# A paired load of the first two weight tiles, and merged stores of the state rows' last output tiles

## The chip, the core and the metric

The kernel runs on one core of one Trainium2 chip. The core has five engines that work side by side: PE (TensorE, matmuls; its weight loads are listed apart as PEld), DVE (VectorE), ACT (ScalarE), POOL (GpSimd) and SP (SyncE). Transfers between the chip's memory (DRAM) and the on-chip memory (SBUF, 128 partitions) are issued by SP or by ACT, each on a queue of its own, and are carried out by 16 DMA engines that both queues share. The metric is the device time of one execution in microseconds. The kernel before takes 871.06 us, the median of three runs (870.91 to 871.29).

## The reference

Three layers follow one another. The inputs are x (batch 8, heads 8, 512 tokens, width 64) and a state (8, 8, 32, 64).

```python
# attention both ways between x and the state
a  = softmax(x @ state.T / 8);   xread = a @ state      # 512 rows per batch and head
a2 = softmax(state @ x.T / 8);   sread = a2 @ x         # 32 rows per batch and head
x = concat([xread, sread], axis=2)                      # -> (8, 576, 512) after the heads are joined
# layer 1: normalise, two matmuls with a relu between, residual
x = x + relu(((x - mean) / std * g_ln) @ w_ch1) @ w_ch2 # w_ch1 512 x 2048, w_ch2 2048 x 512
# layer 2: a gate from a causal 5-tap convolution along the rows, times a projection
out = (sigmoid(conv5(x)) * (x @ w_val)) @ w_out
```

The output has 576 rows per batch: 512 token rows and, behind them, 32 state rows. All arithmetic is float32; the two weight matrices of layer 1 reach the kernel as 64-bit numbers and are turned into float32 on the chip.

## The kernel before

**Start.** `load_tile` loads one weight tile (128 partitions, 512 numbers of 8 bytes, 4 KB per partition, 512 KB in all) by `load_raw` (line 561). Lines 965 to 972 issue, on SP, the first-layer tiles 0, 1 and 2, then x of batch 0 (1 MB, 8 KB per partition, line 109), then tile 3; ACT's queue carries the state of batch 0 (lines 102 and 104), g_ln (line 970) and the identity matrix (line 971). Each tile is decoded in two halves: `decode_a` (two ACT instructions, lines 573 and 575) and `decode_b` (three DVE instructions, lines 581, 583 and 585).

**Order of the first work.** From line 1087 on, the order of PE, ACT and DVE is written out by hand. PE first runs `WARM` = 30 matmuls on zeros (`fill`, line 1095), which only keep it busy. ACT decodes tiles 0, 1, 2. DVE finishes tiles 0 and 1, computes the state's coefficients (lines 125 and 128), finishes tile 2, and only then turns the scores of batch 0 (lines 221 and 225, which need x) and takes their softmax (lines 233 to 235). After that it finishes tile 3. PE runs 14 more fill matmuls behind the scores and then the column sums over tiles 0 to 3 (`colsum`, line 207). The sums are copied by ACT (line 211) and lead into the first hidden layer (lines 169, 170, 729).

**Steady part.** The batches then go through layer 1 in turn (`segment`), with PE as the engine that has nearly no idle time. Behind the eight batches comes one more segment (index B) that holds the state rows of all batches, 256 rows in two tiles of 128. Layer 2 goes over the same nine segments.

**End.** `out_steps(B)` writes the state rows. Row tile 0 holds batches 0 to 3, row tile 1 batches 4 to 7; in each, 32 partitions belong to one batch. The rows of one batch lie together in DRAM, those of the next batch 576 rows further on. So tile 0 is stored by four transfers of 32 partitions (line 923, alternately on SP and ACT). Tile 1 is computed in two column halves of 256, each evicted by ACT (line 935) and stored by four transfers of 32 partitions (line 938): all on SP for the first half, alternately SP and ACT for the last. The token rows are stored by line 925 in transfers of 512 KB.

Buffers: tiles 0 to 3 go to the four `raw` buffers; the `ahl` buffers (two) are first used by the softmax of batch 0.

Of the kernel before, what the change touches and what calls it, by code (L numbers as in the profile page):

```python
# [11 lines left out]
U32 = mybir.dt.uint32  # L12
# [8 lines left out]
P = 128  # L21
B, H, S, NS, D = 8, 8, 512, 32, 64
DM = H * D
DFF = 4 * DM
KT = DM // P
# [2 lines left out]
BASE = 20000  # L28
HLEAD = 4000
LATE = 500  # L30
WARM = 30
DLEAD = 3000
NQ = 4
QF = NF // NQ
# [10 lines left out]
def tile_kernel(ctx: ExitStack, tc: tile.TileContext, xT, xk, stT, sn, w1, w2, wval, wout, convw, gln, ident, stack, out):  # L45
    nc = tc.nc
# [8 lines left out]
    def sb(shape, dt, tag, bufs=1):  # L55
        cnt[0] += 1
        return main.tile(shape, dt, tag=tag, bufs=BUFS.get(tag, bufs), name=f"{tag}_{cnt[0]}")

    def ps(pool, tag, shape):
        cnt[0] += 1  # L60
        return pool.tile(shape, F32, tag=tag, name=f"{tag}_{cnt[0]}")

    def at_ps(shape):
        return ps(ps_at, "at", shape)
# [12 lines left out]
    def mm3(acc, wh, wl, xh, xl, first, last):  # L77
        nc.tensor.matmul(acc, lhsT=wh, rhs=xl, start=first, stop=False)  # L78
        nc.tensor.matmul(acc, lhsT=wl, rhs=xh, start=False, stop=False)  # L79
        nc.tensor.matmul(acc, lhsT=wh, rhs=xh, start=False, stop=last)  # L80
# [19 lines left out]
    def load_state(b, eng=nc.sync):  # L100
        st_raw = small([P, KT, NS], F32, "st_raw")
        eng.dma_start(out=st_raw, in_=stT[b])
        sn_raw = small([P, 2, D], F32, "sn_raw")
        eng.dma_start(out=sn_raw, in_=sn[b])
        loads[b] = [st_raw, sn_raw]
# [453 lines left out]
    def load_raw(tag, src):  # L559
        r = sb([P, DM, 2], U32, tag)  # L560
        nc.sync.dma_start(out=r, in_=src.bitcast(U32).rearrange("p (n two) -> p n two", two=2))
        return r
# [35 lines left out]
    raws, plain_w2 = {}, {}  # L598

    def load_w1(q):  # L600
        for k in range(KT):
            raws["1", 4 * q + k] = load_raw("raw", w1[q, k])

    def load_w2(f):
        raws["2", f] = load_raw(f"w2_{f}", w2[f * P:(f + 1) * P, :])
# [223 lines left out]
    def ntok(i):  # L829
        return S if i < B else NTS  # L830
# [76 lines left out]
    def out_steps(i):  # L907
        n = ntok(i)
        hls = gvs.pop(i)
        for t in range(n // P):  # L910
            if i == B and t == 1:
                break
            o = ps(ps_mm, "mm", [P, DM]) if t % 2 else at_ps([P, DM])
            ts = slice(t * P, (t + 1) * P)
            for e in range(KT):
                mm3(o, hls[e][:, 0, ts], hls[e][:, 1, ts], wo[e][:, 0], wo[e][:, 1], e == 0, e == KT - 1)
            if t % 2 == 0:
                ob = sb([P, 2, DM], F32, "hid", 2)
            nc.scalar.copy(ob[:, t % 2], o)
            if i == B:  # L920
                for j in range(4):
                    eng = nc.scalar if j % 2 else nc.sync
                    eng.dma_start(out=out[4 * t + j, S:, :], in_=ob[32 * j:32 * j + 32, t % 2])
            elif t % 2:
                nc.sync.dma_start(
                    out=out[i, (t - 1) * P:(t + 1) * P, :].rearrange("(u p) d -> p u d", p=P), in_=ob
                )
            yield
        if i == B:
            for half in range(2):  # L930
                cols, ts = slice(half * 2 * P, half * 2 * P + 2 * P), slice(P, 2 * P)
                o = at_ps([P, 2 * P]) if half else ps(ps_mm, "mm", [P, 2 * P])
                for e in range(KT):
                    mm3(o, hls[e][:, 0, ts], hls[e][:, 1, ts], wo[e][:, 0, cols], wo[e][:, 1, cols], e == 0, e == KT - 1)
                nc.scalar.copy(ob[:, 1, cols], o)
                for j in range(4):
                    eng = nc.scalar if half and j % 2 else nc.sync
                    eng.dma_start(out=out[4 + j, S:, cols], in_=ob[32 * j:32 * j + 32, 1, cols])

    def chain(*gens):  # L940
        for g in gens:
# [16 lines left out]
    def load_tile(kind, j):  # L958
        if kind == "1":
            tag = f"w2_{j + 6}" if j // 4 == 1 else "raw"  # L960
            raws["1", j] = load_raw(tag, w1[j // 4, j % 4])
        else:
            raws["2", j] = load_raw(f"w2_{j}", w2[j * P:(j + 1) * P, :])

    load_tile("1", 0)
    load_state(0, nc.scalar)
    load_tile("1", 1)
    load_tile("1", 2)
    load_x(0)
    nc.scalar.dma_start(out=g_sb.rearrange("p k o -> p (k o)"), in_=gln)  # L970
# [116 lines left out]
    with tc.manual_schedule(engines={mybir.EngineType.PE}):  # L1087
# [5 lines left out]
        def fill(n):  # L1093
            for _ in range(n):
                nc.tensor.matmul(warm_ps, lhsT=warm[:, :P], rhs=warm, start=True, stop=True)

        fill(WARM)
        sc0 = [ps(ps_acc, f"acc{2 + u}", [P, S]) for u in range(2)]
# [40 lines left out]
    with tc.manual_schedule(engines={mybir.EngineType.PE}):  # L1139
        segment(1, 8, NF, S, (2, 0), chain(quiet(2), attention_steps(2)))  # L1140
        for b in range(2, B):
            segment(b, 0, NF, S, (b + 1, 0) if b + 1 < B else None, background(b))
        segment(B, 0, NF, NTS, None, before_phase_b())
        at_prio(clock[0] + 16000)
        run_pending()
        bg = x2_steps(1)
        for _ in val_steps(0):
            next(bg, None)
            next(bg, None)
        for i in range(B + 1):  # L1150
            if i + 2 < B:
                load_x2(i + 2)
            bg = x2_steps(i + 2)
            for _ in chain(val_steps(i + 1) if i < B else (), out_steps(i)):
                next(bg, None)
            for _ in bg:
                pass
# [46 lines left out]
```

## Time and profile before

| | |
|---|---|
| median of three runs | 871.06 us |
| the profiled execution's own time | 870.83 us |
| its span, first to last instruction | 868.9 us |
| PE busy | 862.1 us, 99% of the span |
| DVE, ACT, POOL busy | 587.7, 369.7, 199.4 us |
| DMA: moved, mean rate | 72.80 MB, 84 GB/s |

The page of the profile gives busy times and the chain of work that ended last. For this change two short stretches matter: the first 22 us, read from the timeline, the waits and a table of windows, and the last 7 us, read from the timeline, the DMA view and a table of windows. A timeline line gives the start, the length, the engine (SPq and ACTq are the instruction streams that issue transfers), the line of the program, the operation, the tile written and read, the shape and the count; where an engine stood idle, the idle time and what ended it stand in brackets.

### The profile page before, as it was taken

The numbers are of one execution on the slowest core, as the hardware profiler recorded it, in microseconds if no ns is written. First come the engines' busy times: TensorE is split into PE (matmuls) and PEld (weight loads), VectorE is DVE, ScalarE is ACT, GpSimd is POOL, SyncE is SP. The second block draws the span as 40 slices with busy tenths as digits, with TensorE's granted clock in tenths as the row PEclk, the third lists the DMA queues.
The fourth block names the chain that finished last, engine by engine and source line by source line (L and its number), as shares of the span: only waits on it lengthen the run. The fifth ranks groups of instructions, "written<-read, shape, count | busy, mean of one in ns | idle before, by whom it ended". The sixth has DMA issues, their size and how long they took to land.

```text
span 868.9 us, 12589 instructions
## 1 busy us (share of the span) xinstructions
PE 862.1 (99%) x4941; PEld 661.2 (76%) x4942; DVE 587.7 (68%) x995; ACT 369.7 (43%) x696; POOL 199.4 (23%) x162
## 2 busy tenths in 40 slices
PE   9999999999999999999999999999999999999998
PEld 3367767677777777778777777777899888888886
DVE  6999983874746754563674566353389799988870
ACT  5965942233333332432332343132256465455432
POOL 0020200013135133312513422252201223322100
PEclk9999999999999999999999999999999999999999
DMA  9925200321312221230231103010140212223212
GB/s 360 406 85 154 95 29 0 123 79 51 100 53 77 81 72 42 69 99 19 76 98 52 49 11 67 1 49 1 51 144 2 98 73 97 73 98 97 91 55 73
DMA packets 35643, 72.80 MB, mean 84 GB/s; under 512 B 11904, under 2 KB 20608, under 8 KB 31488
## 3 DMA queue, kind: packets, MB, share of 16 engines
q1 hardware_dynamic: 34816, 71.60, 23.9%
q8 instruction: 39, 0.64, 0.3%
q10 hardware_dynamic: 768, 0.40, 0.2%
q14 instruction: 20, 0.16, 0.1%
HBM read 51.01 MB, written 20.97 MB: 83 GB/s over the span
## 4 chain that ended last, share of the span: by engine, by line
PE 86%; DVE 3%; ACT 1%; DMA 0%; issue 0%; DVEq 0%; ACTq 0%
PE mm L734 18%; PE acc L78 16%; PE acc L79 16%; PE acc L80 16%; PE mm L80 2%; PE mm L78 2%; PE mm L79 2%; PE at L80 2%; PE at L78 2%; PE at L79 2%; PE at L147 2%; PE mm L147 1%; PE at L337 1%; PE acc L397 1%; DVE mb L158 1%; PE at L221 1%
## 5 line engine op out<-in xcount | busy, mean ns | idle before, releaser
L78 PE MATMUL acc<-hid,w 128*128 128x512 f32 (+1 forms) x560 | 212.6, 380 | 0.4 <-DVE x L402 0.2
L79 PE MATMUL acc<-hid,w 128*128 128x512 f32 (+1 forms) x560 | 211.4, 378 | 0.0
L80 PE MATMUL acc<-hid,w 128*128 128x512 f32 (+1 forms) x560 | 211.4, 378 | 0.0
L770 DVE SCALAR_TENSOR_TENSOR hid<-mm,hid 128x512 fp32r<-128x512 f32 (+1 forms) x140 | 91.6, 654 | 156.5 <-ACT hid L763 156.3
L734 PE MATMUL mm<-ahl,m 128*128 128x512 f32 x744 | 194.2, 396 | 0.5
L763 ACT ACTIVATE hid<-mm 128x512 fp32r<-128x512 f32 (+2 forms) x144 | 82.3, 571 | 215.5 <-PE mm L734 196.4
L734 PEld LDWEIGHTS mm<-ahl,m 128*128 128x128 f32 x744 | 137.0, 188 | 47.6 <-DVE mb L158 9.3
L78 PEld LDWEIGHTS acc<-hid,w 128*128 128x128 f32 x560 | 105.3, 188 | 24.7 <-issue 1.7
L80 PEld LDWEIGHTS acc<-hid,w 128*128 128x128 f32 x560 | 105.4, 188 | 20.0
L79 PEld LDWEIGHTS acc<-hid,w 128*128 128x128 f32 x560 | 105.4, 188 | 19.1
L861 DVE SCALAR_TENSOR_TENSOR ahl<-big,cw,ahl 128x511 f32<-128x511 f32 (+3 forms) x128 | 102.1, 843 | 0.3
L74 POOL TENSOR_TENSOR m<-mb,m 128x512 fp32r<-128x512 f32 x50 | 65.0, 1320 | 111.1 <-ACT m L73 111.0
L73 ACT ACTIVATE m<-mb 128x512 fp32r<-128x512 f32 x62 | 39.0, 632 | 80.8 <-DVE mb L158 80.5
L847 POOL TENSOR_TENSOR w<-big,w 128x512 fp32r<-128x512 f32 x24 | 37.9, 1611 | 93.0 <-ACT w L845 93.0
L79 PE MATMUL acc<-w,raw 128*128 128x512 f32 (+1 forms) x144 | 54.3, 377 | 0.0
L80 PE MATMUL acc<-w,raw 128*128 128x512 f32 (+1 forms) x144 | 54.3, 377 | 0.0
L78 PE MATMUL acc<-w,raw 128*128 128x512 f32 (+1 forms) x144 | 54.3, 377 | 0.0
L387 POOL TENSOR_TENSOR rstd<-rstd,nhalf 128x16 f32<-128x16 f32 (+1 forms) x9 | 25.7, 2854 | 114.3 <-DVE rstd L385 114.2
L799 DVE TENSOR_TENSOR t<-acc,t 128x512 f32<-128x512 f32 (+1 forms) x44 | 27.8, 660 | 24.3 <-PE acc L80 24.3
L802 POOL TENSOR_TENSOR x<-t,x 128x512 f32<-128x512 f32 x20 | 25.1, 1287 | 78.7 <-DVE t L799 78.7
L873 ACT ACTIVATE ahl<-ahl 128x512 f32<-128x512 f32 (+1 forms) x36 | 21.6, 608 | 45.6 <-DVE ahl L861 45.3
L902 DVE TENSOR_TENSOR w<-ahl,w 128x512 fp32r<-128x512 f32 (+1 forms) x36 | 30.7, 859 | 13.0 <-ACT w L901 12.8
(202 smaller groups left out, 1258.8 us busy)
## 6 DMA issues: line engine op xcount, KB each, us to landing
w<-in_w SPq DMA_DIRECT2D x20, 512.0 KB, 8.0
big<-in_xT SPq DMA_DIRECT2D x8, 1024.0 KB, 4.9
big<-in_xk SPq DMA_DIRECT2D x8, 1024.0 KB, 5.2
x2d<-x SPq DMA_DIRECT2D x8, 1024.0 KB, 4.2
big<-x2d SPq DMA_DIRECT2D x8, 1024.0 KB, 4.8
out<-hid SPq DMA_DIRECT2D x16, 512.0 KB, 2.8
raw<-in_w SPq DMA_DIRECT2D x12, 512.0 KB, 5.6
a2d<-t SPq DMA_DIRECT2D x48, 64.0 KB, 1.7
```

Of the source, the lines that this page charges most:

```text
L73: a = nc.scalar.activation(hi, src, AF.Copy)
L74: eng.tensor_tensor(lo, src, hi.bitcast(F32), op=ALU.subtract)
L78: nc.tensor.matmul(acc, lhsT=wh, rhs=xl, start=first, stop=False)
L79: nc.tensor.matmul(acc, lhsT=wl, rhs=xh, start=False, stop=False)
L80: nc.tensor.matmul(acc, lhsT=wh, rhs=xh, start=False, stop=last)
L734: nc.tensor.matmul(h, lhsT=m[:, u, w, cols], rhs=ahls[b][:, u, x], start=(i, u) == (0, 0), stop=(i, u) == (2, 1),)
L763: a = nc.scalar.activation(hid[:, 0], h, AF.Relu)
L770: marks["dve"] = nc.vector.scalar_tensor_tensor(hid[:, 1], h, 0.0, hid[:, 0].bitcast(F32), op0=ALU.max, op1=ALU.subtract)
L799: marks["dve"] = nc.vector.tensor_tensor(t, accs[d], rrow, op=ALU.mult)
L847: nc.gpsimd.tensor_tensor(lo, src, hi.bitcast(F32), op=ALU.subtract)
L861: t = nc.vector.scalar_tensor_tensor(g[:, j:], x[:, :n - j], cw_sb[:, k, PAD - j:TAPS - j], g[:, j:], op0=ALU.mult, op1=ALU.add)
L902: a = nc.vector.tensor_tensor(hl[:, 1], gt[:, e], hl[:, 0].bitcast(F32), op=ALU.subtract)
```

## The change

The first two weight tiles come in one transfer: the weights are laid out in DRAM so that one partition's parts of tiles 0 and 1 lie side by side, 8 KB together, and the pair goes to an `ahl` buffer in place of two `raw` ones. The other tiles of this matrix are read from the new layout, still 4 KB per partition. The fill matmuls ahead of the first scores go from 30 to 26. At the end, row tile 0 of the state is stored by one transfer of 128 partitions on SP; of row tile 1, the first half by one transfer of 128 partitions on SP and the last half by two of 64 partitions, one on SP and one on ACT.

```diff
-WARM = 30
+WARM = 26
@@ out_steps
             if i == B:
-                for j in range(4):
-                    eng = nc.scalar if j % 2 else nc.sync
-                    eng.dma_start(out=out[4 * t + j, S:, :], in_=ob[32 * j:32 * j + 32, t % 2])
+                nc.sync.dma_start(out=out[4 * t:4 * t + 4, S:, :], in_=ob[:, t % 2])
...
                 nc.scalar.copy(ob[:, 1, cols], o)
-                for j in range(4):
-                    eng = nc.scalar if half and j % 2 else nc.sync
-                    eng.dma_start(out=out[4 + j, S:, cols], in_=ob[32 * j:32 * j + 32, 1, cols])
+                rows = 2 if half else 4
+                for j in range(0, 4, rows):
+                    eng = nc.scalar if j else nc.sync
+                    eng.dma_start(out=out[4 + j:4 + j + rows, S:, cols], in_=ob[32 * j:32 * (j + rows), 1, cols])
@@ load_tile
-            raws["1", j] = load_raw(tag, w1[j // 4, j % 4])
+            raws["1", j] = load_raw(tag, w1[j // 4, j % 4 // 2, :, j % 2])
...
-    load_tile("1", 0)
+    pair = sb([P, 2, DM, 2], U32, "ahl")
+    nc.sync.dma_start(out=pair.rearrange("p j n two -> p (j n two)"), in_=w1[0, 0].rearrange("p j n -> p (j n)").bitcast(U32))
+    for j in range(2):
+        raws["1", j] = pair[:, j]
     load_state(0, nc.scalar)
-    load_tile("1", 1)
     load_tile("1", 2)
@@ kernel
-        "w1": bits(w1.reshape(KT, P, NQ, S).transpose(2, 0, 1, 3)),
+        "w1": bits(w1.reshape(2, 2, P, NQ, S).transpose(3, 0, 2, 1, 4)),
```

## Rows read from the trace of the kernel before

**Rows 1.** The page: busy share, and shares of the chain that ended last.
```profile
PE 862.1 (99%) x4941; PEld 661.2 (76%) x4942; DVE 587.7 (68%) x995; ACT 369.7 (43%) x696; POOL 199.4 (23%) x162
...
PE 86%; DVE 3%; ACT 1%; DMA 0%; issue 0%; DVEq 0%; ACTq 0%
```

**Rows 2.** Timeline, 0 to 12 us: loads issued, fills, decodes of tiles 0 to 2, scores.
```profile
0.74 1.35 SPq L561 DMA_DIRECT2D raw<-in_w  x3
...
1.28 8.59 PE L1095 MATMUL mm<-m 128*128 128x512 bf16 x30 [1.28 <-DVE m L1090]
...
4.87 0.66 ACT L573 ACTIVATE w<-raw 128x512 f32<-128x512 f32 x1 [1.42 <-DMA raw<-in_w]
4.87 0.34 ACTq L971 DMA_DIRECT2D ident<-in_ident  x1
...
5.09 4.27 PEld L1095 LDWEIGHTS <-m 128*128 128x128 bf16 x20 [0.28 <-issue]
...
5.56 0.43 DVE L581 TENSOR_SCALAR w<-w 128x512 f32<-128x512 f32 x1 [4.34 <-ACT w L573]
...
6.34 0.67 ACT L573 ACTIVATE w<-raw 128x512 f32<-128x512 f32 x1 [0.23 <-DMA raw<-in_w]
...
10.21 0.69 DVE L585 CUSTOM_DVE_ANT_0 w<-raw,w 128x1024 uint16<-128x1024 uint16 x1
...
10.47 1.09 PE L221 MATMUL acc<-big,st_raw 64*32 64x512 f32 x16 [0.61 <-DMA big<-in_xT]
...
11.64 1.31 DVE L225 STREAM_TRANSPOSE t<-acc 128x512 f32<-128x512 f32 x2 [0.73 <-PE acc L221]
```

**Rows 3.** Windows of 1 us: busy per engine, then PEclk, DMA share, GB/s last.
```profile
4.00:5.00 1.00, 1.00 (x4) 0.29 (x2) 0.00 (x0) 0.13 (x1) 0.00 (x0) 1.00 1.08 423
5.00:6.00 1.00, 1.00 (x5) 0.44 (x4) 0.43 (x1) 1.00 (x2) 0.00 (x0) 1.00 1.02 389
...
7.00:8.00 1.00, 1.00 (x7) 0.42 (x5) 0.97 (x3) 0.84 (x3) 0.00 (x0) 1.00 1.01 418
```

**Rows 4.** Timeline, 16 to 19 us: tile 3 on DVE, and what PE and ACT do next.
```profile
16.49 0.69 DVE L585 CUSTOM_DVE_ANT_0 w<-raw,w 128x1024 uint16<-128x1024 uint16 x1
...
17.24 0.30 PEld L207 LDWEIGHTS at<-w,g 128*128 128x128 f32 x2 [0.80 <-DVE w L585]
...
18.38 0.68 ACT L1120 ACTIVATE t<-ident,sbn 128x128 f32<-128x128 f32 x2
...
18.97 0.56 ACT L211 COPY cs<-at 128x512 f32<-128x512 f32 x1
```

**Rows 5.** Windows of 5 us behind it (PE, PEld, DVE, ACT, POOL busy).
```profile
20.00:25.00 5.00, 5.00 (x18) 1.63 (x17) 4.81 (x10) 3.77 (x10) 0.00 (x0) 1.00 1.02 417
25.00:30.00 5.00, 5.00 (x14) 1.82 (x14) 4.33 (x14) 5.00 (x11) 0.00 (x0) 1.00 1.03 409
```

**Rows 6.** Timeline of the end: evictions and stores of the state rows.
```profile
862.84 0.93 SPq L923 DMA_DIRECT2D out<-hid  x2
862.84 0.93 ACTq L923 DMA_DIRECT2D out<-hid  x2
...
864.21 2.72 SPq L938 DMA_DIRECT2D out<-hid  x6
...
865.05 0.37 ACT L935 COPY hid<-at 128x256 f32<-128x256 f32 x1 [0.87 <-PE at L80]
865.46 0.80 ACTq L938 DMA_DIRECT2D out<-hid  x2
```

**Rows 7.** DMA view, 862.8 to 869 us: packets, then issues by size and landing.
```profile
DMA packets 582, 0.54 MB, mean 86 GB/s; under 512 B 193, under 2 KB 449, under 8 KB 582
...
out<-hid SPq DMA_DIRECT2D x6, 32.0 KB, 1.6
```

**Rows 8.** The page, DMA issues: the stores of token rows (line 925).
```profile
out<-hid SPq DMA_DIRECT2D x16, 512.0 KB, 2.8
```

**Rows 9.** Windows of the end; columns as in rows 3.
```profile
861.40:861.90 0.50, 0.50 (x4) 0.42 (x3) 0.00 (x0) 0.00 (x0) 0.00 (x0) 1.00 1.00 373
...
864.00:864.50 0.50, 0.50 (x7) 0.50 (x5) 0.00 (x0) 0.19 (x1) 0.00 (x0) 1.00 1.04 250
...
866.50:867.00 0.50, 0.00 (x0) 0.00 (x0) 0.00 (x0) 0.00 (x0) 0.00 (x0) 1.00 0.58 148
...
868.00:868.90 0.90, 0.00 (x0) 0.00 (x0) 0.00 (x0) 0.00 (x0) 0.00 (x0) 0.95 0.00 0
```

More of the change, by code (lines that the diff above doesn't have):

```diff
@@ L601, in load_w1 @@
         for k in range(KT):
-            raws["1", 4 * q + k] = load_raw("raw", w1[q, k])
+            raws["1", 4 * q + k] = load_raw("raw", w1[q, k // 2, :, k % 2])
     def load_w2(f):
```

## The prediction, made before the result was known

> **What bounds the kernel now.** I read the page first. PE is busy 99% of the span and carries 86% of the chain that ended last; DMA has 0% of it [rows 1]. So the middle of the run is PE's, and the change does not touch it: what comes after the first layer-1 work only moves with its start. Two places are left where this change can make time: the stretch before PE is steadily fed, and the stretch after PE's last matmul. I read them in that order, each from the timeline, and then priced the transfers from the windows and the DMA view.
>
> At the start the reader should see a relay. Tile 0 lands and ACT begins to decode at 4.87; DVE begins at 5.56, and its last instruction of the decode of tile 2 starts at 10.21 and ends at 10.90. It has no gap between. x releases the scores at 10.47 (PE stood idle 0.61), and DVE takes the scores at 11.64 after 0.73 us of idling [rows 2]. So here x is last, and DVE's decode has 0.73 us to spare. From 11.64 DVE runs without a gap until it has finished tile 3, at 16.49 + 0.69 = 17.18, and PE's fourth column sum waits for just that and starts at 17.24 [rows 4]. DVE therefore sets the start of everything behind it.
>
> At the end, PE is done at 865.0, ACT has evicted the last half at 865.42, and ACT issues at 865.46, but SP issues six transfers one after the other from 864.21 for 2.72 us, so its last one starts near 866.5 [rows 6]; it lands 1.6 us later, near 868.1 [rows 7]. The span ends at 868.9. Here SP's issuing is the bound.
>
> **The front: the pair.** Before, ACT and DVE work on tile 0 while tile 1 is in flight. Tile 1 is released at 6.34 [rows 2], and both tiles in one transfer cannot be released before about then. Larger packets help little: x, with 8 KB per partition, moves at 418 GB/s at a DMA share of 1.01, the 4 KB tiles at 389 to 423 at 1.02 to 1.08 [rows 3], which is 414 against some 385 at a full share; that is 0.17 us for 1 MB. I take the release at 6.2. ACT's first decode, and with it DVE's, slips by 6.2 - 4.87 = 1.33 us. DVE's block of 10.90 - 5.56 = 5.34 us then ends at 5.56 + 1.33 + 5.34 = 12.23, past the 11.64 at which the scores are there now (11.5 if x gains its 0.1). DVE loses 0.55 us, its spare time is gone, and what is late is DVE instead of x. ACT is not late: its six decode instructions at 0.67 us [rows 2] end by 10.3, and it then waits for DVE anyway. The ends for this term are -0.1 (only x's gain counts) and +1.33 (nothing is spare); I take +0.55, because the spare time is a row.
>
> Behind it nothing gives the 0.55 us back: tile 3 passes from DVE to PE, then ACT copies the sums at 18.97, with two other instructions just before [rows 4], and in the next windows DVE has 4.81 and ACT 5.00 of 5 us busy [rows 5]. So PE's steady part starts 0.55 us later, and the end with it.
>
> **The front: smaller edits.** One issue less on SP is some 0.45 us (three take 1.35 [rows 2]), but the DMA share is at 1.0 [rows 3], so an earlier issue waits in the queue: nothing. The identity matrix's issue on ACT stands beside the first decode, at 4.87 [rows 2], and may slip with it by 1.33 us; it is read at 18.38 [rows 4], so that is covered. The last twenty fills take 4.27 us, so four fewer are 4 x 0.21 = 0.85 us of PE work [rows 2]; they end at 9.0 in place of 9.87, ahead of a wait for x until 10.4: nothing, and the idle time grows from 0.6 to 1.4 us. The pair's buffer is free again at 10, long before the second use of `ahl`, and tiles loaded later into `raw` find their buffers no later than before: nothing.
>
> **The end: fewer issues.** SP has one issue for the last half in place of two behind four others; it and ACT's start at 865.46. If the merged transfers still run on all 16 engines, each queue brings 4 packets per engine, 8 in all in place of 2. A 1 KB packet takes 1024 B / (148 / 0.58 / 16 GB/s) = 64 ns [rows 9], so six more are 0.4 us, and the last lands at 865.46 + 1.6 + 0.4 = 867.4: 0.7 us sooner than 868.1.
>
> **The end: how many engines.** This is the term that decides, and no row shows it. What the rows show is how the old transfers were dealt out. In the last 6 us there are twelve of 32 partitions, and the packets under 512 B are 193: 16 closings for each of the twelve and one over. The 1 KB packets are 449 - 193 = 256, that is 8 x 32 [rows 7]. So every transfer was closed on 16 engines, with two whole rows on each: whole, equal shares of the outermost count, 32. The merged store has an outermost count in DRAM of 4 batches, and of 2 in the last half. Whole shares of that go to 4 engines and to 2 engines. I take whole shares, since nothing in the trace was dealt any other way; the other end is 16 engines, above.
>
> The price: in full flow an engine moves 373 / 16 = 23.3 GB/s [rows 9], 88 ns for 2 KB; I take 46 ns for 1 KB, a little over half. Row tile 0 is then 32 packets of 2 KB on each of four engines, 2.8 us; the first half 32 packets of 1 KB, 1.5 us. The last half puts 32 packets from SP and 32 from ACT on two engines: 2.9 us if both queues get the same two, and I take it that they do, as the dearer of the two cases that leave a share whole. All of it adds up on those engines, since SP's packets stand in line: 7.2 us. The fixed part of a landing is 2.8 - 16 x 0.088 = 1.4 us, from the 512 KB stores [rows 8]. From the first issue at 862.84 [rows 6] the last landing is at 862.84 + 1.4 + 7.2 = 871.45, against 868.1: +3.35 us. Bounds inside this case: 128 KB per engine if the two last halves lie on different engines, 862.84 + 1.4 + 5.8 = 870.0, so +1.9; and 160 KB at the slow rate of the 32-partition stores, 250 / 1.04 / 16 = 15 GB/s or 68 ns per KB [rows 9], 10.9 us, so +7.0.
>
> The Trainium skill, "DMA: Bandwidth & Descriptors", section "Why a DMA increments its semaphore by 16 and not by 1", says of transfers issued from SP and ACT that the number of engines is the largest one up to 16 that divides the slowest counts of both patterns, and that these are the lowest-numbered engines. The closings of [rows 7] agree for a count of 32; for 4 and 2 no run here shows it. By that rule the sum is the one with 4 and 2 engines, by the same page's rule on small transfers it is the one with 16 (below).
>
> **The sum.** The profiled execution took 870.83 us, 1.93 around a span of 868.9. With +0.55 and +3.35 the span is 872.8 and the execution 874.7; the median of the runs is 0.23 above the profiled one, so 874.9.
>
> **The rivals.** (1) The merged stores run on 16 engines. Then the end gains 0.7 and the front loses 0.55: 870.9, no measurable change and not slower. It decides from about eight engines on: 64 KB each are 2.9 us, landing at 862.84 + 1.4 + 2.9 = 867.1, before the last half's issue allows. For it: the SBUF side still has 128 partitions. Against it: no row of a transfer whose shares were cut. The Trainium skill, "DMA: Bandwidth & Descriptors", section "Rules for kernel authors", speaks for it with its advice to merge small transfers, because under 64 KB most of the time is overhead; the 1.6 us for 32 KB beside 2.8 us for 512 KB agree [rows 7, 8].
>
> (2) The front costs nothing, because the pair lands early enough to fit DVE's 0.73 us: 874.3 with the stores on few engines. It needs the pair by 5.6, when one tile took until 4.87 and the DMA share is already 1.0 [rows 2, 3].
>
> (3) PE's clock falls in the longer idle time before the scores, and the next 3 us of fills and the first column sums run at 1.2 in place of 2.4 GHz: scores 1.1 us later, some 1.7 in all, 876.6. Against it: at the end the granted clock is still 1.00 until the last tenth of 868.0 to 868.9 [rows 9], over 3 us after the last matmul, and here the idle time is 1.4 us.
>
> (4) The order of ACT, DVE and SP behind the hand-written part is planned anew from changed due times; nothing in the trace prices it, and I allow 1 us either way.
>
> **How the numbers follow.** Few engines at the end with the front's loss (with or without rivals 2 and 4): 0.74. Sixteen engines: 0.20. A fallen clock on top: 0.04. Something that gains more than the 0.7 us: 0.02. About 0.2%, 1.7 us, is what a measurement of this kernel can tell from no change. Slower by more than that takes 872.8; the first case passes it but for its low corner (870.0 at the stores, no loss in front), the second does not. Slower 0.74, same 0.22, faster 0.04. The likeliest case alone is 872.9 to 878.3 (bounds +1.9 to +7.0, with the front's); to leave out no more than 2 in 10 the range must reach into rival 1, to 870.7.
>
> **What would show it.** The pair: ACT's first decode near 6.2, DVE taking the scores near 12.2 with no idle time before, PE's fourth column sum near 17.8. The stores: closing packets of the four merged transfers, 4 + 4 + 2 + 2 if I am right and 64 if not; in the windows behind 865 a low DMA share with a long tail; the merged store of tile 0 landing 4 us and more after its issue. I am wrong if the last landing comes within 2 us of the last issue, or if DVE still idles before the scores.

## The result and the profile after

The changed kernel takes 876.79 us (median of six executions, 876.62 to 876.85), against 871.08 us for the kernel before beside it: a ratio of 1.0065 (95% interval 1.0052 to 1.0078), 5.7 us slower. The profiled execution took 876.85 us with a span of 874.9 us; before it was 870.83 and 868.9. The 6.0 us by which the spans differ fall into two parts. PE's last matmul starts at 865.52 in place of 864.74, 0.78 us later, and from there to the end of the span it is 9.38 us in place of 4.16, 5.22 us more.

The page of after: the busy times and the chain that ended last, as in [rows 1].

```profile
PE 860.9 (98%) x4937; PEld 660.7 (76%) x4938; DVE 588.2 (67%) x995; ACT 369.5 (42%) x696; POOL 199.9 (23%) x162
...
PE 86%; DVE 2%; ACT 1%; issue 0%; DVEq 0%
```

PE has four fills less and runs the same instructions otherwise; the chain still is PE's and says nothing of a tail of 9 us that lies in transfers. The page alone would not have shown the cause.

The timeline of after at the start (start, length, engine, line, operation, tiles, idle time and what ended it), to be read beside [rows 2] and [rows 4]:

```profile
6.09 0.66 ACT L573 ACTIVATE w<-ahl 128x512 f32<-128x512 f32 x1 [1.90 <-DMA ahl<-in_w]
...
10.29 1.09 PE L221 MATMUL acc<-big,st_raw 64*32 64x512 f32 x16 [1.27 <-DMA big<-in_xT]
...
12.06 1.31 DVE L225 STREAM_TRANSPOSE t<-acc 128x512 f32<-128x512 f32 x2
...
17.65 1.12 PE L207 MATMUL at<-w,g 128*128 128x512 f32 x2 [0.56 <-DVE w L585]
```

The pair lands at 6.09 and ACT's first decode starts 1.22 us later than before. DVE takes the scores at 12.06 with no idle time in front, and PE's fourth column sum starts at 17.65, 0.41 us later than the 17.24 of [rows 4]. PE keeps this distance until about 100 us. There it grows by 0.84 us. Timeline of after, ACT near 78 us and PE near 101 us:

```profile
78.19 1.29 ACT L73 ACTIVATE m<-mb 128x512 fp32r<-128x512 f32 x2 [3.26 <-DVE mb L158]
79.38 0.58 ACT L763 ACTIVATE hid<-mm 128x512 fp32r<-128x512 f32 x1
...
101.40 1.65 PE L734 MATMUL mm<-ahl,m 128*128 128x512 f32 x6 [0.97 <-DVE hid L770]
```

The same of the kernel before:

```profile
76.04 0.60 ACT L763 ACTIVATE hid<-mm 128x512 fp32r<-128x512 f32 x1 [1.53 <-PE mm L734]
...
78.76 1.14 ACT L73 ACTIVATE m<-mb 128x512 fp32r<-128x512 f32 x2
...
100.15 1.66 PE L734 MATMUL mm<-ahl,m 128*128 128x512 f32 x6
```

Before, ACT ran the relu (L763) first and the two copies `m<-mb` behind it, and PE started the L734 matmuls without a wait. Now the copies stand ahead of the relu on ACT and wait 3.26 us for DVE. Some of the loss comes back later: the distance is 1.25 us at 101 us and 0.78 us at the end.

Timeline of after at the end (line 921 is now the store of row tile 0, line 937 the stores of the halves), beside [rows 6]:

```profile
863.63 0.70 SPq L921 DMA_DIRECT2D out<-hid  x1
...
864.80 1.97 SPq L937 DMA_DIRECT2D out<-hid  x2
...
865.52 0.28 PE L80 MATMUL at<-w,w 128*128 128x256 f32 x1
...
865.84 0.37 ACT L933 COPY hid<-at 128x256 f32<-128x256 f32 x1 [1.06 <-PE at L80]
866.24 1.37 ACTq L937 DMA_DIRECT2D out<-hid  x1
```

PE's last matmul in the kernel before:

```profile
864.74 0.28 PE L80 MATMUL at<-w,w 128*128 128x256 f32 x1
```

Windows of after at the end; columns as in [rows 3], so the last three are PEclk, DMA share and GB/s:

```profile
864.50:865.00 0.50, 0.50 (x6) 0.50 (x6) 0.00 (x0) 0.28 (x1) 0.00 (x0) 1.00 0.04 12
865.00:865.50 0.50, 0.50 (x6) 0.50 (x5) 0.00 (x0) 0.00 (x0) 0.00 (x0) 1.00 0.38 37
865.50:866.00 0.50, 0.30 (x3) 0.10 (x1) 0.00 (x0) 0.16 (x1) 0.00 (x0) 1.00 0.29 12
866.00:866.50 0.50, 0.00 (x0) 0.00 (x0) 0.00 (x0) 0.21 (x1) 0.00 (x0) 1.00 0.07 12
866.50:867.00 0.50, 0.00 (x0) 0.00 (x0) 0.00 (x0) 0.00 (x0) 0.00 (x0) 1.00 0.27 61
...
868.00:868.50 0.50, 0.00 (x0) 0.00 (x0) 0.00 (x0) 0.00 (x0) 0.00 (x0) 1.00 0.26 98
...
871.00:872.00 1.00, 0.00 (x0) 0.00 (x0) 0.00 (x0) 0.00 (x0) 0.00 (x0) 0.50 0.14 48
...
873.00:874.00 1.00, 0.00 (x0) 0.00 (x0) 0.00 (x0) 0.00 (x0) 0.00 (x0) 0.50 0.06 19
```

The DMA share is that of 16 engines, so it counts them. 0.26 x 16 is four engines, at 98 GB/s; 0.14 x 16 is two, at 48 GB/s. Before, the rows of the end show shares of 1.04 (from 864.0) and 0.58 (from 866.5) [rows 9]. From 865.5 to 866.5 only 12 GB/s move, at shares of 0.29 and 0.07. A packet is counted whole in the window in which it starts, so the two are read together: about three engines are occupied for a microsecond, and what moves is an eighth of the 98 GB/s that move later.

DMA view of after from 866 us to the end, beside [rows 7]:

```profile
DMA packets 381, 0.49 MB, mean 55 GB/s; under 512 B 12, under 2 KB 268, under 8 KB 381
```

The packets under 512 B are the closings, 12: four for each of the two 128-partition stores and two for each of the two 64-partition stores.

### The profile page after: what moved, and what is told of

It is laid out like the page before. It is cut to its first block, busy times and chain, and to the rows that moved or that the text cites. A ratio compares the mean times of both kernels' runs of the same rounds, so it can differ in the third digit from the quotient of the medians.

```text
span 874.9 us, 12571 instructions
## 1 busy us (share of the span) xinstructions
PE 860.9 (98%) x4937; PEld 660.7 (76%) x4938; DVE 588.2 (67%) x995; ACT 369.5 (42%) x696; POOL 199.9 (23%) x162
## 4 chain that ended last, share of the span: by engine, by line
PE 86%; DVE 2%; ACT 1%; issue 0%; DVEq 0%
PE mm L734 18%; PE acc L78 16%; PE acc L79 16%; PE acc L80 16%; PE mm L80 3%; PE mm L78 3%; PE mm L79 3%; PE at L80 2%; PE at L78 2%; PE at L79 2%; PE at L147 2%; PE mm L147 1%; PE at L337 1%; PE acc L397 1%; DVE mb L158 1%; PE at L221 1%
## 5 line engine op out<-in xcount | busy, mean ns | idle before, releaser
L770 DVE SCALAR_TENSOR_TENSOR hid<-mm,hid 128x512 fp32r<-128x512 f32 (+1 forms) x140 | 91.7, 655 | 156.3 <-ACT hid L763 156.1
L734 PE MATMUL mm<-ahl,m 128*128 128x512 f32 x744 | 194.1, 396 | 1.3 <-DVE hid L770 1.0
L734 PEld LDWEIGHTS mm<-ahl,m 128*128 128x128 f32 x744 | 137.0, 188 | 48.4 <-DVE mb L158 9.3
L763 ACT ACTIVATE hid<-mm 128x512 fp32r<-128x512 f32 (+2 forms) x144 | 82.2, 571 | 213.4 <-PE mm L734 194.1
L74 POOL TENSOR_TENSOR m<-mb,m 128x512 fp32r<-128x512 f32 x50 | 64.9, 1317 | 111.1 <-ACT m L73 111.0
```

The costliest lines, as they stand in the source:

```text
L74: eng.tensor_tensor(lo, src, hi.bitcast(F32), op=ALU.subtract)
L734: nc.tensor.matmul(h, lhsT=m[:, u, w, cols], rhs=ahls[b][:, u, x], start=(i, u) == (0, 0), stop=(i, u) == (2, 1),)
L763: a = nc.scalar.activation(hid[:, 0], h, AF.Relu)
L770: marks["dve"] = nc.vector.scalar_tensor_tensor(hid[:, 1], h, 0.0, hid[:, 0].bitcast(F32), op0=ALU.max, op1=ALU.subtract)
```

## The experiments

Each experiment is timed beside the kernel before on the same chip; a ratio is that of the medians, with its 95% interval. "PE's distance" is how much later PE starts the same matmul than in the profile of before.

### Front alone, stores alone

`e1_front` is the changed kernel with the stores of the kernel before (lines 921 to 923 and 936 to 938 there); `e2_stores` is the kernel before with the changed stores alone:

```diff
-                for j in range(4):
-                    eng = nc.scalar if j % 2 else nc.sync
-                    eng.dma_start(out=out[4 * t + j, S:, :], in_=ob[32 * j:32 * j + 32, t % 2])
+                nc.sync.dma_start(out=out[4 * t:4 * t + 4, S:, :], in_=ob[:, t % 2])
...
-                for j in range(4):
-                    eng = nc.scalar if half and j % 2 else nc.sync
-                    eng.dma_start(out=out[4 + j, S:, cols], in_=ob[32 * j:32 * j + 32, 1, cols])
+                rows = 2 if half else 4
+                for j in range(0, 4, rows):
+                    eng = nc.scalar if j else nc.sync
+                    eng.dma_start(out=out[4 + j:4 + j + rows, S:, cols], in_=ob[32 * j:32 * (j + rows), 1, cols])
```

> The changed front alone (paired load, 26 fills), with the stores of the kernel before. Theory: DVE, late by the pair, costs 0.4 us at PE's fourth column sum (17.65 against 17.24), and the order of ACT that is planned anew near 75 us another 0.4 us, so PE's last matmul ends near 865.8 against 865.0 and the time is 871.9 us (+0.8). Rival: the front costs nothing and the whole loss of 5.7 us is the stores': 871.1 us.

> The merged stores alone, with the front of the kernel before. Theory (few engines): PE's last matmul ends at 865.0 as before, 12 closing packets in place of 192 for the state's stores, and the end is as late behind PE as in the changed kernel, 9.1 us in place of 3.9: 876.0 us (+4.9 to +5.0). Rival (the stores are only hurt together with the later front): less than +4.

Measured: `e1_front` 871.81 us against 871.24 (1.0007, 0.9998 to 1.0016); `e2_stores` 875.91 us against 871.24 (1.0054, 1.0041 to 1.0068). DMA view of `e2_stores`, 863.5 to 875 us:

```profile
DMA packets 396, 0.52 MB, mean 46 GB/s; under 512 B 12, under 2 KB 268, under 8 KB 396
```

With the old front the tail is the same as in after: 12 closings, and from PE's last matmul (864.73) to the end of the span (874.1) 9.37 us. The two parts add up: +0.6 and +4.7 us, 5.2 of the 5.7. So the stores are the change's cost; the front is small, and its interval reaches below 1.

### Same stores, other rows: is it the engines or the merging?

`e10_rows128` is `e2_stores` with another target. It issues the same four transfers of the same bytes from the same tiles, but into 128 or 64 consecutive token rows, so that the outermost count in DRAM is 128 or 64 in place of 4 or 2. It leaves out the state rows of all eight batches, not only of batches 4 to 7 as its expectation says, and writes over token rows of batches 0 and 1.

```diff
-                nc.sync.dma_start(out=out[4 * t:4 * t + 4, S:, :], in_=ob[:, t % 2])
+                nc.sync.dma_start(out=out[0, :P, :], in_=ob[:, t % 2])
...
-                    eng.dma_start(out=out[4 + j:4 + j + rows, S:, cols], in_=ob[32 * j:32 * (j + rows), 1, cols])
+                    eng.dma_start(out=out[1, 32 * j:32 * (j + rows), cols], in_=ob[32 * j:32 * (j + rows), 1, cols])
```

> The kernel before with the changed stores, but the four merged transfers go to 128, 128, 64 and 64 consecutive rows of token rows in place of the state rows (so the state rows of batches 4 to 7 are left out and token rows are written over): as many issues, as many bytes and as large packets as in the changed kernel, and an outermost count of 128 or 64 in DRAM in place of 4 or 2. Theory (the number of engines sets the price): 64 closings in place of 12, the last landing about 2 us behind the last issue, near 867.5, span 868.2 to 868.6, 870.1 to 870.5. Rival (merging by itself is dear, through longer issues or a late start of the flow): a span of 871 us or more, over 873.

Measured: 870.35 us against 871.09 (0.9991, 0.9981 to 1.0001), span 868.6. DMA view of `e10_rows128` from 862.5 us, the packets and the store of tile 0 with its landing time:

```profile
DMA packets 453, 0.55 MB, mean 90 GB/s; under 512 B 65, under 2 KB 321, under 8 KB 452
...
out<-hid SPq DMA_DIRECT2D x1, 256.0 KB, 2.4
```

Timeline of `e10_rows128`, its first and its last issue:

```profile
862.85 0.34 SPq L921 DMA_DIRECT2D out<-hid  x1
...
865.47 0.56 ACTq L937 DMA_DIRECT2D out<-hid  x1
```

Window of `e10_rows128` behind the store of tile 0; columns as in [rows 3]:

```profile
863.50:864.00 0.50, 0.50 (x6) 0.50 (x6) 0.00 (x0) 0.37 (x1) 0.00 (x0) 1.00 0.60 213
```

The closings are 64 (and one of another transfer). Tile 0 moves at 213 GB/s about a microsecond behind its issue and lands after 2.4 us, and the tail from PE's last matmul is 3.85 us in place of 9.37. Merging is therefore not dear by itself: with 16 engines it is no dearer than the twelve small stores. The gain that the prediction's first rival gave it is not told from none: 0.74 us by the medians with an interval that reaches 1.0001, and 0.31 us by the tails (3.85 against 4.16). What is dear is the small outermost count. The edit changes the pattern in DRAM along with the count, from rows of several batches to plain rows; that the number of engines follows from the count in a plain transfer too is shown by `e7_rows` below. The issuing instruction is shorter as well: 0.34 us on SP for tile 0 in place of 0.70, and 0.56 us on ACT for the last half in place of 1.37.

### Each merged store by itself

`e3_tile0` takes the first half of the edit of `e2_stores` alone: tile 0 in one store. `e4_last` merges the stores of the last half alone:

```diff
-                for j in range(4):
-                    eng = nc.scalar if half and j % 2 else nc.sync
-                    eng.dma_start(out=out[4 + j, S:, cols], in_=ob[32 * j:32 * j + 32, 1, cols])
+                rows = 2 if half else 1
+                for j in range(0, 4, rows):
+                    eng = nc.scalar if half and j else nc.sync
+                    eng.dma_start(out=out[4 + j:4 + j + rows, S:, cols], in_=ob[32 * j:32 * (j + rows), 1, cols])
```

> Only the store of row tile 0 merged (one transfer of 128 partitions, outermost count 4); all of tile 1 stored by 32 partitions as before. Theory: 4 closings for it, its packets flow on four engines, full flow starts only some 2.5 us after the issue, and it closes near 868.1 to 868.9; the later stores have their packets on these four engines behind it, so the span is 869.5 to 870. If the late start of the flow came from the next merged transfer issued behind it, its packets flow from 1.0 us after the issue and close near 866.6, and the span is within 0.3 of 868.9. If it ran on 16 engines: 16 closings, span 868.7.

> Only the last half merged (two transfers of 64 partitions, outermost count 2, one on SP, one on ACT); tile 0 and the first half stored by 32 partitions as before. Theory: 2 + 2 closings, both queues on the same two engines, 64 packets of 46 ns on each, 2.9 us; with a flow that starts 2.5 us after the issue at 865.46 the span is 871.8 (+2.9), with one that starts after 1.0 us it is 870.3 (+1.4). If the queues had different pairs of engines, 1.5 us less. On 16 engines: 868.1 (-0.8).

Measured: `e3_tile0` took 873.5 us in a single execution (before 871.24), with 6.65 us from PE's last matmul to the end and a span of 871.7, where 869.5 to 870 was expected: a miss. `e4_last` took 873.11 us against 871.24 (1.0022, 1.0013 to 1.0031), with 6.75 us and a span of 871.7, where 871.8 was expected. The size was as expected, but the way to it was not quite: SP's merged store is the last of five issues that run from 864.74 to 867.32, and the expectation had it at 865.46. Timeline of `e3_tile0` (line 936 is the stores of the halves):

```profile
863.15 0.70 SPq L921 DMA_DIRECT2D out<-hid  x1
...
864.32 5.20 SPq L936 DMA_DIRECT2D out<-hid  x6
```

DMA view of `e3_tile0`, issues with their landing times:

```profile
out<-hid SPq DMA_DIRECT2D x6, 32.0 KB, 4.4
out<-hid ACTq DMA_DIRECT2D x2, 32.0 KB, 4.0
```

The six small stores on SP now take 5.20 us to issue in place of 2.72 [rows 6], and the 32 KB stores, ACT's too, land 4.0 to 4.4 us after their issue (medians) in place of 1.6 [rows 7]. I read this so: each of them has a share on the engines that still work on tile 0, and has not landed before that share is through. That a transfer on four engines holds up the transfers behind it that use all sixteen is what the landings show. The expectation had this, but not that SP's issuing is held up with them: its 2.48 us more are as much as the tail grew (6.65 - 4.16 = 2.49). Why the issuing takes longer, no row shows.

### The rule for the number of engines, away from the end

`e7_rows` cuts three stores of 128 token rows in the middle of layer 2 into pieces of 124 + 4, 62 + 62 + 4 and 31 + 96 + 1 rows: plain transfers, one row per partition, under other work.

```diff
+                cuts = {3: (0, 124, 128), 4: (0, 62, 124, 128), 5: (0, 31, 127, 128)}.get(i)
+                if cuts and t == 3:
...
+                    for lo, hi in zip(cuts, cuts[1:]):
+                        nc.sync.dma_start(out=out[i, t * P + lo:t * P + hi, :], in_=ob[lo:hi, 1])
```

> A probe in the middle of layer 2, where nothing waits for the stores: the last row tile of batches 3, 4 and 5 is stored by plain two-dimensional transfers of 124 + 4, 62 + 62 + 4 and 31 + 96 + 1 rows, everything else as before. Theory (as many engines as divide the outermost count): closings 4 + 4, 2 + 2 + 4 and 1 + 16 + 1, and 84 to 88 ns per packet of 2 KB on each engine. Two readings of the late flow of the merged stores: if it comes from many rows per engine, these flow late as well, some 1 us after the first packets; if it comes from the three-dimensional pattern of the merged stores, they flow at once. The time stays at 871.1 to 871.4.

Measured: 871.79 us in a single execution; the time is not the point. Windows of `e7_rows` behind the 62-row stores, which are issued from 808.92; columns as in [rows 3]:

```profile
810.00:811.00 1.00, 1.00 (x6) 0.84 (x5) 1.00 (x2) 0.00 (x0) 0.00 (x0) 1.00 0.10 23
...
814.00:815.00 1.00, 1.00 (x6) 0.79 (x6) 1.00 (x2) 0.57 (x2) 0.00 (x0) 1.00 0.14 53
```

DMA view of `e7_rows`, 808.5 to 817 us:

```profile
DMA packets 137, 0.28 MB, mean 33 GB/s; under 512 B 8, under 2 KB 8, under 8 KB 136
```

Windows of `e7_rows`: the first of the 124-row store, two in which the 96-row store flows, and one with the 31-row store alone:

```profile
792.00:793.00 1.00, 1.00 (x6) 0.84 (x5) 1.00 (x3) 0.02 (x1) 0.00 (x0) 1.00 0.25 92
...
825.00:826.00 1.00, 1.00 (x6) 0.80 (x6) 1.00 (x4) 0.00 (x0) 0.00 (x0) 1.00 0.90 250
826.00:827.00 1.00, 1.00 (x6) 0.84 (x5) 1.00 (x3) 0.00 (x0) 0.00 (x0) 1.00 0.30 72
...
828.00:829.00 1.00, 1.00 (x6) 0.84 (x5) 1.00 (x3) 0.00 (x0) 0.00 (x0) 1.00 0.06 25
```

Timeline of `e7_rows`, the issues of the 124 + 4 and of the 62 + 62 + 4 rows:

```profile
787.69 0.68 SPq L929 DMA_DIRECT2D out<-hid  x2
...
808.92 1.15 SPq L929 DMA_DIRECT2D out<-hid  x3
```

The shares count two engines (0.14), four (0.25) and one (0.06): the largest divisors of 62, 124 and 31 up to 16. The closings of the 62 + 62 + 4 rows are 2 + 2 + 4 = 8. So a prime or nearly prime number of rows does the same as a few batches, in a plain transfer too. Two engines need some four microseconds here to come from 23 to 53 GB/s, with their share at 0.10 to 0.14 all the while: the slow start is not owed to the pattern of the merged stores. Nor does it go with few engines alone. The 124-row store, whose bytes moved only some 4 us after its issue, behind a load of 1 MB, ran at 92 GB/s on four engines in its first window. The 96-row store, on 16 engines, was slow: 250 GB/s at a share of 0.90 and 72 at 0.30 are 17 and 15 GB/s per engine, against 23.3 in full flow [rows 9]. In `e10_rows128`, also on 16 engines, tile 0 was not slow. What makes the first packets slow I did not find out. The long issues are not owed to few engines alone either: here two take 0.68 us and three take 1.15, below 0.4 us each on average.

### The front taken apart

`e8_fills30` has the pair and the layout with 30 fills, `e9_fills26` is the kernel before with 26 fills and nothing else; `e5_two_loads` has the layout and the `ahl` buffer with 26 fills, but two loads of 4 KB per partition. All three keep the old stores.

```diff
-    nc.sync.dma_start(out=pair.rearrange("p j n two -> p (j n two)"), in_=w1[0, 0].rearrange("p j n -> p (j n)").bitcast(U32))
-    for j in range(2):
-        raws["1", j] = pair[:, j]
+    def load_half(j):
+        nc.sync.dma_start(out=pair[:, j], in_=w1[0, 0, :, j].bitcast(U32).rearrange("p (n two) -> p n two", two=2))
+        raws["1", j] = pair[:, j]
+    load_half(0)
     load_state(0, nc.scalar)
+    load_half(1)
     load_tile("1", 2)
```

The diff is that of `e5_two_loads` against `e1_front`. `e8_fills30` is `e1_front` with `WARM = 30`, and `e9_fills26` is the kernel before with `WARM = 26`.

> The pair in one transfer, but 30 fills as before; stores as before. ACT's order near 75 us is that of the kernel before. Theory: PE's fourth column sum +0.4 (17.65), no second step near 100 us, PE's last matmul +0.4 or less, 871.5 us. Rival (the second step comes from the pair's late start and not from the order): PE's shift still grows by 0.8 near 100 us.

> The kernel before with WARM = 26 in place of 30 and nothing else. Theory (four fills fewer change the order that is planned for ACT behind the hand-written part, two copies of m<-mb are put ahead of the relu near 76 us): PE shows no shift against the kernel before up to 99 us beyond the scatter of x's landing, a step of about 0.8 us near 100 us, and 0.4 to 0.6 us of it at the end: 871.4 to 871.6. Rival (the pair's loads and the weights' new layout move ACT's order, the number of fills has no part in it): no step near 100 us, 871.0.

> The changed front with 26 fills, the new layout and the pair's buffer, but tiles 0 and 1 in two transfers of 4 KB per partition; stores as before. ACT's planned order near 75 us is that of the changed kernel (two evictions of m ahead of a relu of hid). Theory: tile 0 is released near 4.9 again, DVE takes the scores at 11.64 and PE's fourth column sum starts at 17.24 (+0.0), but the order still costs 0.8 us behind 85 us, of which 0.4 come back by 650: PE's last matmul +0.4, 871.5 us. Rival (the order costs nothing, all of the front's loss is the pair's): 871.1.

Measured: `e8_fills30` 871.05 us against 870.96 (1.0001, 0.9992 to 1.0010); `e9_fills26` 871.84 against 871.09 (1.0010, 1.0001 to 1.0019); `e5_two_loads` 871.85 against 870.96 (1.0011, 1.0002 to 1.0020). The first is lower than expected, the other two are higher, by 0.2 to 0.5 us. Timeline of `e8_fills30`, ACT and PE:

```profile
76.25 0.60 ACT L763 ACTIVATE hid<-mm 128x512 fp32r<-128x512 f32 x1 [1.53 <-PE mm L734]
...
78.98 1.15 ACT L73 ACTIVATE m<-mb 128x512 fp32r<-128x512 f32 x2
...
100.36 1.66 PE L734 MATMUL mm<-ahl,m 128*128 128x512 f32 x6
```

The same of `e9_fills26`, with two lines of DVE:

```profile
78.03 1.29 ACT L73 ACTIVATE m<-mb 128x512 fp32r<-128x512 f32 x2 [3.25 <-DVE mb L158]
...
78.70 1.35 DVE L74 TENSOR_TENSOR m<-mb,m 128x512 fp32r<-128x512 f32 x2
...
79.23 0.58 ACT L763 ACTIVATE hid<-mm 128x512 fp32r<-128x512 f32 x1
...
100.47 0.68 DVE L770 SCALAR_TENSOR_TENSOR hid<-mm,hid 128x512 fp32r<-128x512 f32 x1
...
101.21 1.65 PE L734 MATMUL mm<-ahl,m 128*128 128x512 f32 x6 [0.93 <-DVE hid L770]
```

DVE of the kernel before, the same two places:

```profile
80.97 1.28 DVE L74 TENSOR_TENSOR m<-mb,m 128x512 fp32r<-128x512 f32 x2
...
99.41 0.68 DVE L770 SCALAR_TENSOR_TENSOR hid<-mm,hid 128x512 fp32r<-128x512 f32 x1
```

The number of fills alone puts the copies ahead of the relu. With 30 fills and the pair, ACT's order is that of before, and PE's distance is 0.20 us at 17.5 us, 0.21 at 100 and 0.05 at the end. With 26 fills and the old loads it is 0.25 us at 17.5, 1.06 at 101 and 0.98 at the end. The fills are not slower and are not missed by PE; what costs is that an order that is planned for ACT and DVE came out otherwise 70 us later. In the whole trace of `e9_fills26` this is the one place where the order on PE, ACT, DVE or POOL differs from before, but for the fills: ACT's two copies, and DVE's two instructions behind them (L74), stand ahead of a relu and of an L770. DVE carries the loss on. It is busy for 26.60 of the 27 us from 74 to 101 in the kernel before, so it has nothing to make it up from: its instructions are 0.27 us late at 77.3, 0.84 at 83.6 and 1.06 from 89.7 to 100.47, and the L770 there is what PE waits for. The step goes with this order in every kernel: 0.8 us in the four with 26 fills (after, `e1_front`, `e5_two_loads`, `e9_fills26`), at most 0.1 in the other eight, which have 30.

The profiled execution of `e5_two_loads` was one of two in ten that took about 873 us; the other eight took 871.5 to 871.9. Its timeline at the scores:

```profile
10.84 1.76 PE L221 MATMUL acc<-big,st_raw 64*32 64x512 f32 x16 [2.30 <-DMA big<-in_xT]
```

Windows of `e5_two_loads`; columns as in [rows 3]:

```profile
11.00:12.00 1.00, 1.00 (x16) 0.02 (x3) 0.26 (x1) 0.00 (x0) 0.00 (x0) 0.57 1.01 401
12.00:13.00 1.00, 1.00 (x10) 0.20 (x3) 0.37 (x1) 0.90 (x2) 0.00 (x0) 0.50 1.03 410
```

x came 0.55 us later than in after and the fills ended 0.48 us sooner (8.54 against 9.02), so PE idled 2.30 us, and the granted clock fell to 0.5, from 2.4 to 1.2 GHz, from shortly after 11 us until past 14: the scores took 1.76 us in place of 1.09. PE's distance is 1.88 us at the fourth column sum and 1.5 from 21 us to the step at 100. That is the prediction's third rival. In after, the idle time was 1.27 us and the clock stayed.

### A store order that is no slower

`e6_spread` is the kernel before with the first half's four stores alternately on SP and ACT.

```diff
-                    eng = nc.scalar if half and j % 2 else nc.sync
+                    eng = nc.scalar if j % 2 else nc.sync
```

> The kernel before with the first half's four stores of tile 1 alternately on SP and ACT, as the last half's are; every transfer stays at 32 partitions. Theory: 16 closings for each, SP's last issue starts near 865.9 in place of 866.5, and the span is 868.3, the time 870.6 us (-0.5), too little for the interval to show. Rival: ACT's two more issues delay its last eviction (865.05) or its own issues, and the time is 871.1 or more.

Measured: 870.15 us against 870.96 (0.9992, 0.9983 to 1.0000). Timeline of `e6_spread`:

```profile
864.24 1.74 ACTq L938 DMA_DIRECT2D out<-hid  x4
```

Its span from PE's last matmul is 4.08 us against 4.16, so the profile shows hardly any gain at the end; ACT's four issues now end last, at 865.98. PE's last matmul came 0.82 us earlier in this execution, which the edit does not touch: x landed early, and the scores started at 9.93 in place of 10.47, which is 0.54 of it. It is the lowest time measured, but the interval reaches 1, and it can't be told from the kernel before.

## Why the prediction was right, and where it was off

The direction and the mechanism came out as argued: 876.79 us measured, 874.9 predicted. For the profiled execution the prediction made 874.7; it took 876.85, and the 2.15 us between them are 0.23 at the front and 1.87 at the end, but for rounding. Two of its sums are a little off: 12.23 - 11.64 is 0.59 and not 0.55, and 871.06 + 0.55 + 7.0 is 878.6 and not 878.3. Neither changes a reading.

**What bounds the kernel, and the two places.** Right. No other stretch changed, but for the step at 100 us and the part of it that comes back later.

**The pair.** The steps were right: release at 6.09 (6.2 predicted), scores on DVE at 12.06 without idle time (12.2), fourth column sum at 17.65 (17.8). But 0.41 us in one profile is not a price. In the eight profiles with the old loads (before, `e2_stores`, `e3_tile0`, `e4_last`, `e6_spread`, `e7_rows`, `e9_fills26`, `e10_rows128`) the scores start between 9.93 and 11.18, the fourth column sum 6.76 to 6.78 us behind them, and DVE always idles before the scores, 0.43 to 1.58 us: there the landing ahead of the scores sets the start, and it moves from one execution to the next. The profile of before, with 10.47, is the second earliest of the eight; five of them have the column sum at 17.41 to 17.65. With the pair DVE sets the start, and the column sum is at 17.44 (`e8_fills30`), 17.50 (`e1_front`) and 17.65 (after), no later than those five. `e8_fills30` puts the pair at +0.1 us, with an interval of -0.7 to +0.9. The term of 0.55 failed where it took the spare time of one execution, and an early one, for that of all.

**Fills at nothing.** Wrong: +0.75 us by the medians of `e9_fills26` (0.1 to 1.7 by its interval). The named cover, the wait for x, was there (1.27 us idle), but the cost lay where no row of the front could show it, in the order planned for ACT and DVE. The fourth rival had named that and allowed 1 us either way; 0.8 us of it came true. It stood in for the pair's missing 0.45, so the sum for the front (0.55) was nearly right, by 0.57 us in `e1_front`, by luck and not by its reason.

**Fewer issues.** The gain of 0.7 us, which held for 16 engines only, is not shown: `e10_rows128` is 0.74 us below the kernel before by the medians, but the interval of the ratio (0.9981 to 1.0001) allows no gain too, and the two profiles' tails differ by 0.31 us.

**How many engines.** Right, and the term that decided: 4 + 4 + 2 + 2 closings. The rule of the Trainium skill, "DMA: Bandwidth & Descriptors", section "Why a DMA increments its semaphore by 16 and not by 1", agrees with these 12, with the 64 of `e10_rows128` and with 62, 124 and 31 rows. The Trainium skill's section "Rules for kernel authors" of the same page, by which merging small transfers pays, goes against the +4.7 us of `e2_stores` and fits `e10_rows128` at most. That advice speaks of overhead, so the prediction's 16 engines did not follow from it.

**The price of few engines.** The mis-sized term: +5.22 us in place of +3.35. The rates were right: 98 to 104 GB/s on four engines and 48 on two were measured, 93 and 47 taken (23.3 each). Both last halves did go to the same two engines. The first bytes also moved no later than I took it: 6 KB came before 865.0, within 1.4 us of the issue at 863.63. What failed is the step from the fixed part of 1.4 us, read from 512 KB stores on 16 engines, straight to full flow. From 865.0 to 866.5 the windows carry (37 + 12 + 12) x 0.5 = 31 KB, where 93 GB/s are 140 KB; from 866.5 to 868.0 they carry (61 + 61 + 90) x 0.5 = 106 KB. The 143 KB that lack are 1.5 us at 93 GB/s, of the 1.87 us. The rest, 0.35 us, I can't place. The upper bound of +7.0 held it.

**The rivals.** (1) 16 engines: ruled out by the closings, and `e10_rows128`, which has them, shows no loss. (2) A free front: within the scatter for the pair. (3) The clock: not in after, but in `e5_two_loads` after 2.30 us of idling; PE's lasting distance of 1.5 us there, less the 0.37 us by which x came later than in [rows 2], is 1.1 us, against the 1.7 us that I took. What I held against it, that the clock stayed for over 3 us after the last matmul of before, did not rule it out. (4) The new order: as above.

## What to carry to other kernels

Before merging stores, look at the outermost count of the pattern in DRAM: where it is 4 or 2, the transfer runs on four or two of the sixteen engines, and the DMA share in a table of windows (0.26, 0.14) and the number of closing packets say so at once. A kernel's end has nothing to hide such a transfer, and it also holds up the small transfers behind it that have a share on the same engines, and their issuing. And where a planner orders the instructions, compare the order on each engine after any edit, an edit of idle work included: four dummy matmuls less moved two instructions on each of two other engines 70 us later and cost 0.8 us.

## What the runs showed of the hardware that I had not expected

A store's first packets can be slow. In after, the merged stores carried 12 GB/s from 865.5 to 866.5, at a mean share of 0.18, and 98 GB/s from 868.0 on; in `e7_rows` two engines came from 23 to 53 GB/s in some four microseconds, and 16 engines ran at 15 to 17 GB/s each with 96 rows. It was not seen with the 124 rows on four engines in `e7_rows`, nor with tile 0 on 16 engines in `e10_rows128`, which moved 213 GB/s about a microsecond behind its issue. So it is not a matter of few engines alone. The issuing instruction of the merged stores is longer as well, 0.70 against 0.34 us for 256 KB on SP and 1.37 against 0.56 us for 64 KB on ACT, while in `e7_rows` the plain stores of 124 + 4 and of 62 + 62 + 4 rows took below 0.4 us each and the three of 31 + 96 + 1 rows 1.92 us together. The cause of neither is settled.
